# Expert layer of a three-stage kernel: token blocks in threes with a 15-product scheme in place of pairs with an 11-product scheme

## The chip, the cores and the metric

The kernel runs on one core of a Trainium2 chip. The metric is the device time of one execution in microseconds (us); less is better. The engines are named as in the profile: PE (TensorE matmuls) and PEld (its weight loads), DVE (VectorE), ACT (ScalarE), POOL (GpSimd), SP (the queue that issues the loads and stores).

## The reference

Three layers follow each other on 3072 tokens of width 384: a gated linear attention, a squared-ReLU MLP, and a layer of 8 experts mixed by a Sinkhorn-normalised gate. The change lies in the last one:

```python
def _moe2_ref(x, w_gate, w1, w2):          # x 3072x384, w1 8x384x1024, w2 8x1024x384
    logits = x @ w_gate
    P = np.exp(logits - logits.max())
    for _ in range(8):
        P /= P.sum(1, keepdims=True) + 1e-09
        P /= P.sum(0, keepdims=True) + 1e-09
        P *= N / E
    for e in range(E):
        h = np.maximum(x @ w1[e], 0.0)
        out += P[:, e:e + 1] * (h @ w2[e])
    return out
```

## The kernel before

Everything is laid out with features on the 128 partitions and tokens along the free axis. Attention runs in 24 chunks of 128 tokens, the MLP in 8 blocks of 384 tokens; both are interleaved, and each MLP result is stored to DRAM (`x2d`). The expert layer then takes the tokens in 3 pairs of blocks of 512 (`TB`), and for each pair all 8 experts. An expert has 1024 hidden features, taken in 4 steps of 256 (two blocks of 128). A step is numbered g, 96 in all; two steps make a super step q, 48 in all.

Each fp32 factor is split into a high part and the rest (`hi` by a cast on ACT, `lo` by a subtraction on DVE), and one block product (128x128 weights by 128x512 tokens) is three matmuls: hi·hi, hi·lo, lo·hi (`triple`, line 730).

First products (x by w1): a step needs 2 token blocks x 3 blocks of the width x 2 hidden blocks = 12 block products. A bilinear scheme (a Strassen-like one, `PROD`) does it with 11, on sums and differences of blocks of x (`x_sum`, once for a pair of token blocks) and of w1 (`w_sum` on POOL, lines 702 to 704, once a step). Its results are shared among outputs. So a PSUM bank is read while its sum is not finished (`take`, a copy by ACT, line 748), the next product is added to the same bank, and `part` and `whole` (DVE, lines 752 and 757) add the snapshots to the other banks. The finished hidden block goes through ReLU into `hi` (`hid_hi`, ACT, line 765) and `lo` (`hid_lo`, DVE, line 770).

Second products (h by w2, `second`, line 781): at the end of a super step, six groups (2 token blocks x 3 blocks of the output width) of 12 matmuls, each group summed in one of two PSUM banks. `weigh` (DVE, line 804) multiplies a finished group by the gate, `gather` (POOL, line 813) adds it to the accumulator in SBUF, which is stored after the last expert.

The weights of a step come by two loads (`ldwa`, `ldwc`) into two raw buffers; `w2_hi` (ACT, line 715) and `w2_lo` (DVE, line 719) split them. For the tokens, `ldx` loads a block from `x2d`; `x_hi` (line 678) and `x_lo` (line 681) split the blocks and the sums. The Sinkhorn steps (lines 1043 to 1062, DVE, POOL and a small matmul) run beside the first super steps; the gate is needed only from the second expert on, and the first expert's accumulators are scaled afterwards by `scale0` (POOL, line 807).

The order on every engine is fixed when the program is built: each operation is a step with an engine, a duration, a due time and its needs (`add`), and `Plan.order` plays them through and writes the instructions down in that order. At run time each engine executes its list in order and waits, by semaphores, for what the next instruction needs; nothing overtakes.

Of the kernel before, what the change touches and what calls it, by code (L numbers as in the profile page):

```python
# [37 lines left out]
NPAIR = NT // (2 * TB)  # L38
NST = NEF // 2
W1C = 10  # L40
WCOL = 2 * D
LAG = 2
NWP = 10
WARM_AT = 1.3
WARM_MARGIN = 0.45
W_AT = 6.0
CV_AT = 14.0
# [20 lines left out]
class Plan:  # L68
# [9 lines left out]
    def __init__(self):  # L78
        self.steps = {}

# [8 lines left out]
    def order(self):  # L89
# [11 lines left out]
        def arm(n):  # L101
            eng, _, due, _, needs, _, start = steps[n]
            at = max([ends[d] + (0.0 if steps[d][0] == eng else self.HOP) for d in needs] + [start])
            ready.setdefault(eng, []).append((at, due, n))
# [5 lines left out]
        while any(ready.values()):  # L110
            best = None
            for eng, c in ready.items():
                if not c:
                    continue
                t = max(free.get(eng, 0.0), min(x[0] for x in c))
                at, due, n = min((x for x in c if x[0] <= t), key=lambda x: (x[0] if eng == "dma" else x[1], x[0], str(x[2])))

                soon = min((x[0] for x in c if t < x[0] < t + min(steps[n][1], self.LOOK.get(eng, 0.0)) and x[1] + self.URGENT < due), default=t)
                if soon > t:
                    t = soon  # L120
                    at, due, n = min((x for x in c if x[0] <= t), key=lambda x: (x[1], x[0], str(x[2])))
                if best is None or t < best[0]:
                    best = (t, eng, (at, due, n))
# [4 lines left out]
            ends[n] = free[eng] + steps[n][5]  # L128
# [9 lines left out]
    def emit(self, between=None):  # L138

        free = 0.0  # L140
        for n in self.order():
            eng, dur, _, fn, _, lag, _ = self.steps[n]
            if eng == "pe" and between:
                at = self.ends[n] - lag - dur
                between(free, at)
                free = at + dur
            fn()


def body(tc, fkq, v, wm, wa, wc, gate, seqs, out):  # L150
# [8 lines left out]
    ps_e = ctx.enter_context(tc.tile_pool(name="ps_e", bufs=2, space=PSUM))  # L159
# [18 lines left out]
    right = ExitStack()  # L178
    rpool = lambda name, bufs: right.enter_context(tc.tile_pool(name=name, bufs=bufs, side="right", reuse_waits="tile"))
    wb = rpool("wb", 1)  # L180
    x1p = rpool("x1p", 2)
# [353 lines left out]
    def products_in(i, w, xx):  # L535
        ps = eps[i] = ps_e.tile([128, BT], F32, tag="e1", name="e1")
# [88 lines left out]
    NSTEP = NPAIR * NE * NST  # L625
    NSUP = NSTEP // 2

    def close_right():
# [6 lines left out]
        pools["pb"] = new("pbp", 2, side="right")  # L635
        pools["c"] = new("ps_c", 1, space=PSUM)
        pools["o"] = new("ps_o", 2, space=PSUM)
        pools["xr"] = new("xrp", 1, side="right")
# [6 lines left out]
    T_E1, T_E2 = 7.5, 16.3  # L645
# [6 lines left out]
    X, xr, x2r = {}, {}, {}  # L652

    def ldx(p, t):
        x2r[p, t] = pools["xr"].tile([128, KD, TB], F32, tag=f"x{t}", name="xraw") if p else rawp.tile([128, KD, TB], F32, tag="raw", name="xraw")
        lo, hi = (2 * p + t) * TB, (2 * p + t + 1) * TB
        while lo < hi:
            j = lo // BT
            end = min(hi, (j + 1) * BT)
            o = (2 * p + t) * TB  # L660
            sp.dma_start(out=x2r[p, t][:, :, lo - o:end - o], in_=x2d[j][:, :, lo - j * BT:end - j * BT])
            lo = end

# [12 lines left out]
    def x_hi(p, n):
        X.setdefault(p, {})[n] = (pools["xr"] if n == 0 and p == 1 else pools["x"]).tile([128, 2, (3, 2, 4)[n], TB], F32R, name="xd" if n == 0 and p == 1 else f"x{n}")
        act.copy(out=X[p][n][:, 0], in_=x_src(p, n))

    def x_lo(p, n):  # L680
        dve.tensor_tensor(out=X[p][n][:, 1], in0=x_src(p, n), in1=X[p][n][:, 0].bitcast(F32), op=ALU.subtract)

    def xop(p, name):
        n, k = {"a11": (0, 0), "a12": (0, 1), "a13": (0, 2), "a22": (1, 0), "a23": (1, 1),
                "s1": (2, 0), "s2": (2, 1), "s3": (2, 2), "s4": (2, 3)}[name]
        return [X[p][n][:, l, k, :] for l in range(2)]


    W2 = {}

    def ldwa(g):
        raws["a", g] = rawp.tile([128, W1C, 128], F32, tag="raw", name="rawa")
        sp.dma_start(out=raws["a", g][:, 0:6], in_=wa[g % (NE * NST)])

    def ldwc(g):
        raws["c", g] = rawp.tile([128, WCOL], F32, tag="raw", name="rawc")
        sp.dma_start(out=raws["c", g], in_=wc[g % (NE * NST)])

    def w_sum(g):
        r = raws["a", g]  # L700

        pool.tensor_tensor(out=r[:, 6:8], in0=r[:, 1:3], in1=r[:, 0:2], op=ALU.subtract)  # L702
        pool.tensor_tensor(out=r[:, 8], in0=r[:, 2], in1=r[:, 6], op=ALU.subtract)
        pool.tensor_tensor(out=r[:, 9], in0=r[:, 3], in1=r[:, 8], op=ALU.subtract)  # L704

    def w2src(g, k):
        if k == "c":
            return raws["c", g], WCOL
        r = raws["a", g].rearrange("p a b -> p (a b)")
        return (r[:, 0:WCOL], WCOL) if k == "a" else (r[:, WCOL:], 512)  # L710

    def w2_hi(g, k):
        W2[g, k] = wpool.tile([128, 2, WCOL], F32R, tag=f"w{(3 * g + 'abc'.index(k)) % NWP}", name="w2")
# [7 lines left out]
    def wop(g, name):  # L721
        c = {"b11": 0, "b22": 2, "b21": 3, "b13": 4, "b23": 5, "t1": 6, "t3": 7, "t2": 8, "t4": 9}[name]
        w, c = (W2[g, "a"], c) if c < 6 else (W2[g, "b"], c - 6)
        return [w[:, l, c * 128:(c + 1) * 128] for l in range(2)]

    bank, snap, vs, hs = {}, {}, {}, {}

    def triple(ps, w, x, start, stop):
        for n, (a, b) in enumerate(((0, 0), (0, 1), (1, 0))):
            pe.matmul(ps, w[a], x[b], start=start and n == 0, stop=stop and n == 2, skip_group_check=True)  # L730


    PROD = {"p1": ("a", (("b11", "a11"),)), "p2": ("b", (("b21", "a12"), ("b13", "a13"))),
            "p6": ("a", (("t2", "s2"),)), "p5": ("c", (("t1", "s1"),)), "p3": ("d", (("b22", "s4"), ("b23", "a13"))),
            "p7": ("a", (("t3", "s3"),)), "p22": ("c", (("b23", "a23"),)), "p4": ("e", (("t4", "a22"), ("b13", "a23")))}

    def product(g, name):
        k, ops = PROD[name]
        p = g // (NE * NST)
        fresh = name in ("p1", "p2", "p5", "p3", "p4")  # L740
        if fresh:
            bank[g, k] = ps_e.tile([128, TB], F32, tag="e1", name="e1") if k in "ab" else pools["c"].tile([128, TB], F32, tag=k, name="e2")
        for n, (w, x) in enumerate(ops):
            triple(bank[g, k], wop(g, w), xop(p, x), fresh and n == 0, True)

    def take(g, n):
        snap[g, n] = pools["x"].tile([128, TB], F32, tag=f"s{n}", name=f"s{n}")
        act.copy(out=snap[g, n], in_=bank[g, "a"])  # L748

    def part(g):  # L750
        vs[g, "t"] = pools["v"].tile([128, TB], F32, tag="t", name="t")
        dve.tensor_tensor(out=vs[g, "t"], in0=bank[g, "c"], in1=snap[g, 2], op=ALU.add)  # L752

    def whole(g, k):
        other = {"b": lambda: snap[g, 1], "d": lambda: vs[g, "t"], "c": lambda: snap[g, 3], "e": lambda: snap[g, 3]}[k]()
        vs[g, k] = pools["v"].tile([128, TB], F32, tag="v", name="v", bufs=3)
        dve.tensor_tensor(out=vs[g, k], in0=bank[g, k], in1=other, op=ALU.add)  # L757

    TF = {"b": (0, 0), "d": (0, 1), "c": (1, 1), "e": (1, 0)}

    def hid_hi(g, k):
        t, f = TF[k]
        f += 2 * (g % 2)
        hs[g // 2, t, f] = pools["h"].tile([128, 2, TB], F32R, tag=f"h{t}{f}", name="h")
        act.activation(out=hs[g // 2, t, f][:, 0], in_=vs[g, k], func=ACTF.Relu)  # L765

    def hid_lo(g, k):
        t, f = TF[k]
        h = hs[g // 2, t, f + 2 * (g % 2)]
        dve.scalar_tensor_tensor(out=h[:, 1], in0=vs[g, k], scalar=0.0, in1=h[:, 0].bitcast(F32), op0=ALU.max, op1=ALU.subtract)  # L770

    acc, ob, sc, pbt = {}, {}, {}, {}

    def second(q, t, m):
        ob[q, t, m] = pools["o"].tile([128, TB], F32, tag="o", name="o")
        for f in range(4):
            w = W2[2 * q + f // 2, "c"]
            c = (f % 2) * D + m * 128
            h = hs[q, t, f]
# [481 lines left out]
```

## Time and profile before

| | |
|---|---|
| three timed runs | 2098.16, 2093.79, 2095.75 us; median 2095.75 |
| profiled execution, first to last instruction | 2092.6 us |
| PE busy | 2059.8 us (98%), 10558 matmuls |
| DVE busy | 1308.6 us (63%) |
| ACT busy | 882.4 us (42%) |
| POOL busy | 640.9 us (31%) |
| mean granted TensorE clock | 0.994 of full speed |

The page gives no other time of the profiled execution than its span; the three timed runs lie 1.2 to 5.6 us above it. A busy time is the union of the records of an engine's instructions. A matmul's record (389 ns for 512 columns) is longer than the distance from one matmul to the next, because they overlap; the distance is read from stretches with a known number of matmuls.

### The profile page before, as it was taken

The page shows a single profiled execution, that of the slowest core. Times are in us where ns is not written, and L with a number is a line of the kernel's source. Part 1 is how long each engine was busy: PE and PEld are TensorE (multiplying, and loading weights), DVE is VectorE, ACT ScalarE, POOL GpSimd, SP SyncE. Part 2 cuts the span into 40 slices and gives each one's busy share as a digit, 9 for nine tenths or more (in the row PEclk, how much of TensorE's full clock was granted, in tenths as well). Part 3 has the DMA queues.
Part 4 walks back from the last instruction along what each step waited for, and adds up shares of the span by engine and source line. Part 5 has one row for each costly group of instructions (what it writes and reads, how often), then busy time and mean ns, then how long its engine had stood idle before and what let it go on. Part 6 is the DMA issues. An engine that isn't in the chain of part 4 may idle for free.

```text
span 2092.6 us, 27588 instructions
## 1 busy us (share of the span) xinstructions
PE 2059.8 (98%) x10558; PEld 1732.4 (83%) x10558; DVE 1308.6 (63%) x1999; ACT 882.4 (42%) x1519; POOL 640.9 (31%) x647
## 2 busy tenths in 40 slices
PE   8889999999999999999999999999999999999998
PEld 5579999999977888888888888888888888888887
DVE  8963444332576665667675665667666665665665
ACT  5644544445643343343343343343343343343341
POOL 4420111100124333334332333334332333333331
PEclk9999999999999999999999999999999999999999
DMA  7522222210212211121221111212112211111210
GB/s 284 176 74 66 78 89 70 69 32 18 87 31 78 71 56 56 61 86 56 71 86 56 61 56 56 71 56 86 61 56 86 71 56 56 61 56 56 71 46 32
DMA packets 55114, 148.75 MB, mean 71 GB/s; under 512 B 6333, under 2 KB 15549, under 8 KB 54973
## 3 DMA queue, kind: packets, MB, share of 16 engines
q1 hardware_dynamic: 54972, 146.90, 21.9%
q8 instruction: 85, 1.39, 0.3%
q14 instruction: 57, 0.46, 0.1%
HBM read 135.28 MB, written 9.54 MB: 69 GB/s over the span
## 4 chain that ended last, share of the span: by engine, by line
PE 91%; DVE 6%; DMA 1%; ACT 1%; issue 1%; POOL 0%; SPq 0%; DVEq 0%; POOLq 0%; ACTq 0%
PE o L781 36%; PE e L730 33%; PE e L544 9%; PE a L573 8%; PE pp L360 1%; PE y L408 1%; PE lg L588 1%; DVE h L770 1%; DVE cv_t L1006 1%; PE y L416 1%; DVE cv_t L1002 1%; DVE cv_t L998 1%; DVE w L298 1%; PE ds L382 1%; DVE w L719 1%; DMA rawa<-in_wa_dram 1%
## 5 line engine op out<-in xcount | busy, mean ns | idle before, releaser
L781 PE MATMUL o<-h,w 128*128 128x512 f32 x3456 | 799.0, 391 | 6.9 <-DVE sc L804 3.9
L781 PEld LDWEIGHTS o<-h,w 128*128 128x128 f32 x3456 | 649.3, 188 | 146.2 <-DVE sc L804 6.6
L730 PE MATMUL e<-x,w 128*128 128x512 f32 x2784 | 648.0, 389 | 0.0
L730 PEld LDWEIGHTS e<-x,w 128*128 128x128 f32 x2784 | 522.1, 188 | 108.3 <-DVE t L752 0.2
L748 ACT COPY s<-e 128x512 f32<-128x512 f32 x288 | 169.1, 587 | 842.5 <-PE e L730 837.6
L813 POOL TENSOR_TENSOR acc<-acc,sc 128x512 f32<-128x512 f32 x258 | 336.6, 1313 | 499.8 <-DVE sc L804 499.7
L804 DVE TENSOR_TENSOR sc<-o,pb 128x512 f32<-128x512 f32 x264 | 181.9, 689 | 372.6 <-PE o L781 341.2
L770 DVE SCALAR_TENSOR_TENSOR h<-v,h 128x512 fp32r<-128x512 f32 x384 | 278.2, 743 | 1.3 <-ACT h L765 1.1
L765 ACT ACTIVATE h<-v 128x512 fp32r<-128x512 f32 x384 | 242.5, 632 | 40.2 <-DVE v L757 40.1
L757 DVE TENSOR_TENSOR v<-e,s 128x512 f32<-128x512 f32 x288 | 198.0, 687 | 78.2 <-ACT w L715 61.5
L702 POOL TENSOR_TENSOR rawa<-rawa 128x256 f32<-128x256 f32 x96 | 79.7, 830 | 506.9 <-DMA rawa<-in_wa_dram 301.9
L544 PE MATMUL e<-x,w 128*128 128x384 f32 x1008 | 198.1, 339 | 0.0
L560 DVE TENSOR_TENSOR lo<-g,hi 128x384 fp32r<-128x384 f32 x112 | 65.6, 585 | 202.1 <-ACT hi L556 201.5
L544 PEld LDWEIGHTS e<-x,w 128*128 128x128 f32 x1008 | 173.9, 188 | 4.8 <-issue 2.4
L573 PE MATMUL a<-hi,w 128*128 128x384 f32 x672 | 171.9, 336 | 0.0
L719 DVE TENSOR_TENSOR w<-rawa,w 128x768 fp32r<-128x768 f32 x192 | 160.1, 834 | 6.3 <-ACT w L715 6.3
L715 ACT CAST w<-rawa 128x768 fp32r<-128x768 f32 x192 | 135.3, 729 | 22.1 <-POOL rawa L704 9.3
L549 ACT ACTIVATE g<-e 128x384 f32<-128x384 f32 x128 | 62.9, 491 | 160.5 <-PE e L544 148.8
L573 PEld LDWEIGHTS a<-hi,w 128*128 128x128 f32 x672 | 120.6, 188 | 0.9
L344 POOL TENSOR_TENSOR kq<-kq,sg 128x512 f32<-128x512 f32 x24 | 31.7, 1322 | 273.7 <-DVE sg L334 135.0
L573 PE MATMUL a<-lo,w 128*128 128x384 f32 x336 | 112.4, 335 | 0.0
L730 PE MATMUL e<-xd,w 128*128 128x512 f32 x384 | 97.4, 389 | 0.0
(110 smaller groups left out, 1529.6 us busy)
## 6 DMA issues: line engine op xcount, KB each, us to landing
rawa<-in_wa_dram SPq DMA_DIRECT2D x96, 384.0 KB, 3.1
rawc<-in_wc_dram SPq DMA_DIRECT2D x96, 384.0 KB, 3.3
raw<-in_wm_dram SPq DMA_DIRECT2D x16, 768.0 KB, 5.4
pb<-ptd SPq DMA_DIRECT2D x24, 512.0 KB, 3.8
fraw<-in_fkq_dram SPq DMA_DIRECT2D x23, 512.0 KB, 4.4
kq<-in_fkq_dram SPq DMA_DIRECT2D x23, 512.0 KB, 4.2
vt<-in_v_dram SPq DMA_DIRECT2D x24, 192.0 KB, 4.7
x2d<-x2t SPq DMA_DIRECT2D x8, 576.0 KB, 2.8
```

The source lines that it names most:

```text
L544: pe.matmul(ps, w[wl][:, k * 128:(k + 1) * 128], xx[:, xl, k, :], start=n == 0, stop=n == 3 * KD - 1)
L573: pe.matmul(acc1[j][m], W[f][wl][:, D + m * 128:D + (m + 1) * 128], g, start=f == 0 and n == 0, stop=f == NF - 1 and n == 2)
L715: act.copy(out=W2[g, k][:, 0, 0:n], in_=src)
L719: dve.tensor_tensor(out=W2[g, k][:, 1, 0:n], in0=src, in1=W2[g, k][:, 0, 0:n].bitcast(F32), op=ALU.subtract)
L730: pe.matmul(ps, w[a], x[b], start=start and n == 0, stop=stop and n == 2, skip_group_check=True)
L748: act.copy(out=snap[g, n], in_=bank[g, "a"])
L757: dve.tensor_tensor(out=vs[g, k], in0=bank[g, k], in1=other, op=ALU.add)
L765: act.activation(out=hs[g // 2, t, f][:, 0], in_=vs[g, k], func=ACTF.Relu)
L770: dve.scalar_tensor_tensor(out=h[:, 1], in0=vs[g, k], scalar=0.0, in1=h[:, 0].bitcast(F32), op0=ALU.max, op1=ALU.subtract)
L781: pe.matmul(ob[q, t, m], w[:, a, c:c + 128], h[:, b], start=f == 0 and n == 0, stop=f == 3 and n == 2)
L804: dve.tensor_tensor(out=dst, in0=ob[q, t, m], in1=pbt[p, e][:, t * TB:(t + 1) * TB], op=ALU.mult)
L813: eng.tensor_tensor(out=acc[p, t, m], in0=acc[p, t, m], in1=sc[q, t, m], op=ALU.add)
```

## The change

A group is now three blocks of 512 tokens, so there are 2 groups, 64 steps and 32 super steps. A step needs 3 x 3 x 2 = 18 block products and makes them with 15. They form five chains: a chain is a PSUM bank that gets up to five products one after the other, and after each product its running sum is read before the next one is added. The reads (`READ`) are 3 copies by ACT and 10 additions or subtractions by DVE; four hidden blocks come out of these sums, two straight from a bank (`DIRECT`). For two of the six hidden blocks `lo` is made on POOL, after ACT has applied ReLU in place (`hid_relu`). Five banks serve the chains, a sixth joins from step 6 on (`lay_banks`). The second products are 9 groups of 12 matmuls, written down in two halves each, in the order of token blocks 0, 2, 1.

The sums of w1 blocks grow from 4 blocks of 128 columns to 11 (three instructions of 256 columns, one of 384, two of 128, on POOL), and the split of the weights from tiles of 768, 512 and 768 columns to three of 640 and one of 768. In all but the first three steps and the first step of a group, the split of an even step's weights waits until the last first product of the step before it. The sums of x blocks are 17 (9 on DVE, 8 on POOL) for a group, the splits 15 blocks; for the second group they wait for the last first product of the first one. Gate rows and some scratch tiles share buffers with others (`w9`, `xe`, `v2`, `v3`).

The planner: an operation marked soft gives way to any other that becomes ready within a short time, the lag of an operation counts only for other engines, and durations are changed.

```diff
-NPAIR = NT // (2 * TB)
+GRP = 3
+NGRP = NT // (GRP * TB)
...
-            ends[n] = free[eng] + steps[n][5]
+            ends[n] = free[eng]
...
-    ps_e = ctx.enter_context(tc.tile_pool(name="ps_e", bufs=2, space=PSUM))
+    ps_e = ctx.enter_context(tc.tile_pool(name="ps_e", bufs=1, space=PSUM))
...
+    PROD = (6, 7, 8, 14, 4, 9, 13, 11, 12, 10, 0, 2, 5, 3, 1)
+    CHAIN = {"c4": (6, 14), "c0": (7, 4, 11, 0, 3), "c2": (8, 9, 12, 2, 1), "c1": (13, 10), "c3": (5,)}
...
+    XSUM = (("6", 6, (1, 1), (2, 0), ALU.add), ("0", 0, (0, 1), 6, ALU.subtract), ("2", 2, (0, 0), 6, ALU.subtract),
...
+    X_POOL = ("14a", "14", "13a", "13", "10a", "10", "5a", "5")
...
+    def x_lo(p, o):
+        dve.tensor_tensor(out=x_dst(p, o, 1), in0=x_src(p, o), in1=x_dst(p, o, 0).bitcast(F32), op=ALU.subtract)
...
-        pool.tensor_tensor(out=r[:, 6:8], in0=r[:, 1:3], in1=r[:, 0:2], op=ALU.subtract)
-        pool.tensor_tensor(out=r[:, 8], in0=r[:, 2], in1=r[:, 6], op=ALU.subtract)
-        pool.tensor_tensor(out=r[:, 9], in0=r[:, 3], in1=r[:, 8], op=ALU.subtract)
+            tt(out=r[:, 6:8], in0=r[:, 1:3], in1=r[:, 0:1].to_broadcast([128, 2, 128]), op=ALU.subtract)
+            tt(out=r[:, 8:10], in0=r[:, 6:8], in1=r[:, 5:6].to_broadcast([128, 2, 128]), op=ALU.subtract)
+            tt(out=r[:, 10:12], in0=r[:, 8:10], in1=r[:, 4:5].to_broadcast([128, 2, 128]), op=ALU.add)
+            return
+        c = raws["c", g]
+        tt(out=c[:, 0:3], in0=r[:, 9:12], in1=r[:, 3:4].to_broadcast([128, 3, 128]), op=ALU.add)
+        tt(out=c[:, 3], in0=r[:, 0], in1=r[:, 5], op=ALU.add)
+        tt(out=c[:, 4], in0=c[:, 1], in1=r[:, 2], op=ALU.add)
...
+    def product(g, o):
+        c = CHAIN_OF[o]
+        if o == CHAIN[c][0]:
+            bank[g, c] = new_bank(g, c)
+        x, w = X[g // GST, o], wop(g, o)
         for n, (a, b) in enumerate(((0, 0), (0, 1), (1, 0))):
+            pe.matmul(bank[g, c], w[a], x[:, b], start=o == CHAIN[c][0] and n == 0, stop=n == 2, skip_group_check=True)
+
+    READ = (("k", 6, "act", 0.49), ("t1a", 7, "dve", 0.61), ("t2a", 8, "act", 0.49), ("t2b", 4, "dve", 0.61), ("t2c", 14, "dve", 0.61),
+            ("t1b", 9, "dve", 0.61), ("t3a", 13, "act", 0.49), ("t0a", 11, "dve", 0.61), ("t0b", 12, "dve", 0.61), ("t0c", 10, "dve", 0.61),
+            ("t3b", 0, "dve", 0.61), ("t3c", 2, "dve", 0.61), ("t1c", 5, "dve", 0.61))
+    OUT = {2: "t2c", 0: "t0c", 3: "t3c", 1: "t1c"}
+    DIRECT = {5: 3, 4: 1}
+    H_POOL = (2, 3)
...
+        else:
+            t = vs[g, name[:2]]
+            op = ALU.subtract if name in ("t2b", "t1b", "t0a", "t0b") else ALU.add
+            dve.tensor_tensor(out=t, in0=t, in1=c, op=op)
...
+    def hid_lo(g, o):
+        h = hs[hid(g, o)]
+        if o in H_POOL:
+            pool.tensor_tensor(out=h[:, 1], in0=hid_src(g, o), in1=h[:, 0].bitcast(F32), op=ALU.subtract)
+        else:
+            dve.scalar_tensor_tensor(out=h[:, 1], in0=hid_src(g, o), scalar=0.0, in1=h[:, 0].bitcast(F32), op0=ALU.max, op1=ALU.subtract)
...
+    T_ORDER = (0, 2, 1)
+    TM = [(t, m) for t in T_ORDER for m in range(KD)]
...
+            needs.append(("p", g1, PROD[-1]) if p else "left")
...
+            if g > 2 and g % 2 == 0 and g % GST:
+                free = [free, ("p", g - 1, PROD[-1])]
...
+            if i:
+                needs.append(("read", g, of_op[CHAIN[c][i - 1]]))
...
+            add(("p", g, o), "pe", 0.68, at(u + 0.68 * j), lambda g=g, o=o: product(g, o), needs, FILL)
```

## Rows read from the trace of the kernel before

**Rows 1.** The page: engines' busy us and shares; chain that ended last, by line.

```profile
PE 2059.8 (98%) x10558; PEld 1732.4 (83%) x10558; DVE 1308.6 (63%) x1999; ACT 882.4 (42%) x1519; POOL 640.9 (31%) x647
...
PE o L781 36%; PE e L730 33%; PE e L544 9%; PE a L573 8%; PE pp L360 1%; PE y L408 1%; PE lg L588 1%; DVE h L770 1%; DVE cv_t L1006 1%; PE y L416 1%; DVE cv_t L1002 1%; DVE cv_t L998 1%; DVE w L298 1%; PE ds L382 1%; DVE w L719 1%; DMA rawa<-in_wa_dram 1%
```

**Rows 2.** Chain of one super step, 700 to 740 us: start, length, what, matmuls.

```profile
706.28 14.96 PE e L730 x66
721.24 16.32 PE o L781 x72
```

**Rows 3.** Groups by line: instructions, busy us, mean ns, idle before.

```profile
L781 PE MATMUL o<-h,w 128*128 128x512 f32 x3456 | 799.0, 391 | 6.9 <-DVE sc L804 3.9 <-DVE acc L798 2.4 <-DVE h L770 0.3
L730 PE MATMUL e<-x,w 128*128 128x512 f32 x2784 | 648.0, 389 | 0.0
L730 PE MATMUL e<-xd,w 128*128 128x512 f32 x384 | 97.4, 389 | 0.0
```

**Rows 4.** Stretches: PE, PEld, DVE, ACT, POOL busy us (instructions), then PE clock.

```profile
706.12:721.08 14.96, 14.96 (x68) 12.39 (x67) 12.96 (x19) 10.81 (x19) 3.60 (x4) 1.00 0.26 89
721.08:737.40 16.32, 16.32 (x74) 13.51 (x73) 7.57 (x12) 1.21 (x3) 8.04 (x8) 1.00 0.14 48
...
616.14:638.42 22.28, 19.80 (x85) 15.48 (x84) 14.10 (x28) 4.32 (x7) 7.22 (x10) 0.92 0.27 76
...
653.38:674.84 21.46, 18.34 (x74) 14.42 (x73) 11.56 (x12) 1.22 (x3) 13.74 (x11) 0.92 0.19 61
...
1065.15:1082.58 17.43, 16.92 (x73) 13.36 (x72) 11.82 (x14) 3.87 (x5) 9.57 (x8) 1.00 0.33 105
```

**Rows 5.** Instructions in order, first products: start, length, engine, operation, [idle before].

```profile
706.12 15.12 PE L730 MATMUL e<-x,w 128*128 128x512 f32 x66
...
707.05 0.59 ACT L748 COPY s<-e 128x512 f32<-128x512 f32 x1 [15.56 <-PE e L730]
...
710.50 0.68 DVE L770 SCALAR_TENSOR_TENSOR h<-v,h 128x512 fp32r<-128x512 f32 x1
711.10 0.68 DVE L757 TENSOR_TENSOR v<-e,t 128x512 f32<-128x512 f32 x1
711.70 0.68 DVE L719 TENSOR_TENSOR w<-rawa,w 128x512 fp32r<-128x512 f32 x1
...
715.51 1.05 POOL L702 TENSOR_TENSOR rawa<-rawa 128x256 f32<-128x256 f32 x1 [7.07 <-DMA rawa<-in_wa_dram]
...
715.87 1.23 DVE L770 SCALAR_TENSOR_TENSOR h<-v,h 128x512 fp32r<-128x512 f32 x1
```

**Rows 6.** Durations of three lines: min/median/max ns.

```profile
L770 DVE SCALAR_TENSOR_TENSOR h<-v,h x384: 641/682/1777, 572.6 to 2071.0; 128x512 fp32r<-128x512 f32 x192
...
L813 POOL TENSOR_TENSOR acc<-acc,sc x258: 1279/1289/2207, 662.5 to 2055.5; 128x512 f32<-128x512 f32 x129
...
L671 DVE TENSOR_TENSOR xs<-xraw,xs x3: 684/1771/1775, 538.4 to 1452.7; 128x512 f32<-128x512 f32 x3
```

**Rows 7.** Instructions in order around two waits of PE.

```profile
619.35 3.01 PE L781 MATMUL o<-h,w 128*128 128x512 f32 x12
...
624.12 0.63 DVE L798 TENSOR_TENSOR acc<-o,acc 128x512 f32<-128x512 f32 x1
...
624.80 4.46 PE L781 MATMUL o<-h,w 128*128 128x512 f32 x12 [2.43 <-DVE acc L798]
...
650.24 10.11 POOL L807 TENSOR_TENSOR acc<-acc,pb 128x512 f32<-128x512 f32 x6
...
654.84 4.38 DVE L770 SCALAR_TENSOR_TENSOR h<-v,h 128x512 fp32r<-128x512 f32 x3
...
662.42 5.78 PE L781 MATMUL o<-h,w 128*128 128x512 f32 x18 [3.05 <-DVE sc L804]
```

**Rows 8.** Groups by line on POOL, the sums of weight blocks.

```profile
L702 POOL TENSOR_TENSOR rawa<-rawa 128x256 f32<-128x256 f32 x96 | 79.7, 830 | 506.9 <-DMA rawa<-in_wa_dram 301.9 <-ACT h L765 162.5 <-DVE v L757 18.8
...
L704 POOL TENSOR_TENSOR rawa<-rawa 128x128 f32<-128x128 f32 x96 | 46.6, 485 | 7.5
```

More of the change, by code (lines that the diff above doesn't have):

```diff
@@ L102, in arm @@
             eng, _, due, _, needs, _, start = steps[n]
-            at = max([ends[d] + (0.0 if steps[d][0] == eng else self.HOP) for d in needs] + [start])
+            at = max([ends[d] + (0.0 if steps[d][0] == eng else self.HOP + steps[d][5]) for d in needs] + [start])
             ready.setdefault(eng, []).append((at, due, n))
@@ new lines, in x_f32, with x_sum, x_src @@
+    def x_f32(p, o):
+        if o in X_OVER:
+            return xraw[p, 0][0][X_OVER[o]]
+        if (p, "t") not in X:
+            X[p, "t"] = x1e.tile([128, 6, TB], F32, tag="x1", name="xt")
+        return X[p, "t"][:, X_SLOT[o]]
+    def x_sum(p, n, eng):
+        _, o, a, b, op = XSUM[n]
+        part = lambda s: xraw[p, s[0]][0][s[1]] if isinstance(s, tuple) else x_f32(p, s)
+        eng.tensor_tensor(out=x_f32(p, o), in0=part(a), in1=part(b), op=op)
+    def x_src(p, o):
+        if o == "89":
+            return xraw[p, 1][1][:, 1:3]
+        if o in SINGLE:
+            t, k = SINGLE[o]
+            return xraw[p, t][0][k]
+        return x_f32(p, o)
@@ L733, in body @@
[L733 to L757, printed above, removed]
@@ L772, in body, with wop @@
-    acc, ob, sc, pbt = {}, {}, {}, {}
[L774 to L779, printed above, removed]
-            for n, (a, b) in enumerate(((0, 0), (0, 1), (1, 0))):
-                pe.matmul(ob[q, t, m], w[:, a, c:c + 128], h[:, b], start=f == 0 and n == 0, stop=f == 3 and n == 2)
+    def wop(g, o):
+        k, c = W_OP[o]
+        return [W2[g, k][:, l, c * 128:(c + 1) * 128] for l in range(2)]
@@ new lines, in body, with lay_banks @@
+    bank, vs, hs = {}, {}, {}
+    RING_AT = 6
+    BANK, FREED = {}, {}
+    def lay_banks():
+        order = ("c4", "c0", "c2", "c1", "c3")
+        now = dict(zip(order, (0, 1, 2, 3, 4)))
+        spare = None
+        last = {}
+        for g in range(NSTEP):
+            if g == RING_AT:
+                spare = 5
+            old = now
+            if spare is None:
+                now = {"c4": old["c4"], "c0": old["c1"], "c2": old["c3"], "c1": old["c0"], "c3": old["c2"]}
+            else:
+                now = {"c4": spare, "c0": old["c4"], "c2": old["c1"], "c1": old["c3"], "c3": old["c2"]}
+                spare = old["c0"]
+            if g == 0:
+                now = old
+            for c in order:
+                BANK[g, c] = now[c]
+                FREED[g, c] = last.get(now[c])
+                last[now[c]] = (g, c)
@@ new lines, in body @@
+        for name, o, eng, dur in READ:
+            needs = [("p", g, o), "right"]
+            if name in READ_AFTER:
+                needs.append(("read", g, READ_AFTER[name]))
+            if name == "k":
+                needs += [("hlo", g - 2, 0)] if g >= 2 else []
+                needs += row_done(1, 2, r) if p and r < 2 else []
+            if name == "t1a":
+                needs += [("hlo", g - 2, 1)] if g >= 2 else []
+                needs += row_done(1, 2, 2) if (p, r) == (1, 0) else []
+            if name in ("t2a", "t3a"):
+                needs += [("hlo", g - 1, 2 if name == "t2a" else 3)] if g else []
+                if g % 2 == 0 and g:
+                    needs += [("ac", g // 2 - 1, *TM[7 if name == "t2a" else 8])]
+            n = PROD.index(o)
+            if name in OUT.values() and name != "t3c":
+                plan.soft.add(("read", g, name))
+            add(("read", g, name), eng, dur, at(u + 0.68 * n + 0.7), lambda g=g, name=name: read(g, name), needs, TAIL)
```

429 lines of the change are left out of this document (271 added, 158 removed).

## The prediction

> **What bounds the kernel now.** I read the page first. PE is busy 98% of the span, no other engine above 63%, and the two lines of the expert layer hold 69% of the chain that ended last [rows 1]. A busy share is an average, so the next view is the chain itself in a quiet stretch: it runs on PE alone, 66 matmuls of first products in 14.96 us and 72 of second products in 16.32 us, with nothing between [rows 2]. That gives the price of a matmul: 31.28 / 138 = 0.2267 us (its record of 389 ns overlaps the next one). The groups by line say that PE never waited ahead of a first product and 6.9 us in all ahead of second ones [rows 3]. So a matmul taken out of the expert layer is worth 0.2267 us as long as the others still keep up, and the whole question is whether they do. DVE is the one to look at: during the first products it is busy 12.96 of 14.96 us, 87%, with POOL at 3.60, 24% [rows 4].
>
> **What is removed.** Before, 96 steps of 11 products of 3 matmuls are 3168, as counted (2784 + 384) [rows 3]. After, 64 steps of 15 products are 2880. The second products stay at 3456: 32 super steps x 9 groups x 12. All have 512 columns and their own weight load, as before, so the price stays. 288 x 0.2267 = 65.3 us go, all from the path that sets the end. A step's first products then take 45 x 0.2267 = 10.2 us, a super step 20.4 + 24.5 = 44.9 us. The weight loads fall from 96 pairs to 64 and stay behind 3 to 4 us of landing in steps of 22 us; nothing is charged.
>
> **What is added to the chains.** A product that adds to a bank has to wait until the sum in it was read. In the new order two products, six matmuls, stand between each product and the next one of its chain. From the start of a product's last matmul to the start of that next one are 7 x 0.2267 = 1.59 us. The read needs: 0.39 for the matmul's record; 0.09 until the reader starts (first product of a step: its third matmul starts at 706.12 + 0.45, ends at 706.96, ACT starts at 707.05); 0.68 for a DVE read [rows 5]; 0.05 until PE goes on (DVE ends at 624.75, PE starts at 624.80) [rows 7]. Sum 1.21, so a slack of 0.38 us, if DVE is free. What is queued behind a late read is everything: the next product stands first in PE's list and nothing overtakes it.
>
> Back to back, DVE starts an instruction of 512 columns every 0.60 us (710.50, 711.10, 711.70) [rows 5], so it can follow reads that come every 0.68 us. In the first products of a super step it has 20 reads, 12.0 us, 8 rests of hidden blocks (`lo`), 4.8 us, and about one split of 768 weight columns, 0.60 x 1.5 = 0.9: 17.7 of 20.4 us, 87%, the same share at which PE did not wait before [rows 4]. The cover is thinner, though. From the fifth product to the thirteenth, reads come with every product but one and leave no hole of 0.6 us; the four `lo` of a step fit only around the turn from one step to the next, where DVE has six products, 4.1 us, for one read and four `lo`, 3.0 us. ACT has 6 copies, 12 ReLU into `hi` and 4 in place, at most 22 x 0.63 = 13.9 of 20.4 us, and is not the bound.
>
> **DVE beside POOL.** A `lo` that started at 715.87, inside a POOL instruction that ran from 715.51 to 716.56, took 1.23 instead of 0.68 us, and ended 0.54 after POOL's end: it did its work after POOL [rows 5]. Three `lo` beside `scale0` took 4.38 us [rows 7], and a sum of two SBUF operands has 1.77 against 0.68 us [rows 6]. The median `lo` shows nothing of it (682 ns), because POOL was rarely busy then. The change alters just that: in the first products of a super step POOL gets 4 `lo` x 1.29 = 5.2 us (length of its other 512-column operation [rows 6]), the weight sums of a step, 3 x 0.83 + 2 x 0.485 [rows 8] + 1.1 (384 columns, between 0.83 and 1.29) = 4.6, and two late accumulations, 2.6: 12.4 of 20.4 us, 61% instead of 24%.
>
> The Trainium skill (SBUF — State Buffer, "Who interferes with whom") says that VectorE and GpSimd share one pair of ports under an exclusive lock, that a VectorE instruction with two SBUF inputs contends with a GpSimd one that reads SBUF, and that the later one waits to the end. The trace agrees (1.23 us, above), and the rule speaks against this change, which puts more work on POOL. Taken at its worst for every `lo` it is the slow rival below.
>
> Price of a chain delay: a `lo` meets a busy POOL 0.61 of the time, has more than the slack left to wait in (1.29 - 0.38) / 1.29 = 0.70 of these cases, and then PE waits 0.46 us on average: 0.61 x 0.70 x 0.46 = 0.2 us. Per super step four DVE `lo` have both inputs in SBUF. All among the tight reads gives 0.8 us; as they are soft and mostly land at the turns, I take 0.3: 32 x 0.3 = 10 us. Lower bound 0, as in the first products before; upper bound, each meets a whole POOL instruction, 4 x 0.91 x 32 = 116 us.
>
> The `lo` that POOL makes: the block out of the twelfth product needs a read 0.68, two ACT operations 0.63 + 0.6, POOL 1.29 and about 0.4 of hand-overs, 3.6 us, and is asked for 3 products (2.0), half a group (1.4) and five matmuls (1.1) later, 4.5. If POOL is in a weight sum, the 0.9 of slack is just used up. I take 0.1 a super step, 3 us, between 0 and 0.5 x 32 = 16.
>
> The weight splits of an even step now wait for the end of the first products. Behind them on ACT and DVE stand only late ReLUs and `weigh` (9 x 0.60 and 8 splits of 0.75 to 0.9 are 11.7 of 24.5 us), so this costs nothing; without that cover the next step's first product would wait.
>
> **The turn to the second group.** 9 sums and 15 splits of x on DVE (24 x 0.60 = 14.4), 8 sums on POOL (10.3), and besides 4 weight splits (3.2), 9 accumulations (11.6) and weight sums (4.6). All of these have two SBUF inputs or run on POOL: 44.1 us if they exclude each other strictly. There are 24.5 us of second products plus 12 products, 8.2, until the last operands are needed: 32.7. So between 0 and 11.4 us late. I take 7, nearer to exclusion as the rows above show it. The two turns of before cost 17.43 - 16.32 = 1.1 us each [rows 4] and go: +5 net, between -2 and +12 (with the reload of a weight buffer that the tokens now borrow).
>
> **The start.** Beside Sinkhorn PE waited 2.43 us, and 3.05 us after `scale0` had held up DVE; the granted clock was 0.92 in both stretches, and the 12 matmuls behind the first wait took 4.46 instead of 3.01 us [rows 4, 7]. After, `scale0` has 9 pieces of 1.69, 15.2 us, beside chains that are tighter, but the gate is needed only after 90 us instead of 63. +2, between -5 and +15. The end is the same chain of last group, `weigh`, sum and store: 0.
>
> **Sum.** -65.3 + 10 + 3 + 5 + 2 = -45.3. Against the profiled span, 2092.6 - 45.3 = 2047.3; the median of the timed runs lies 3.15 above that span, so 2050.
>
> **Rivals.** (1) Nothing waits: the plan knows the DVE and PE distances to 0.01 us, and PE did not wait at 87% before. 2095.75 - 65.3 = 2030, down to 2025 if the start's waits vanish too. Against it: POOL at 61%. (2) DVE's list falls behind in each step: 0.8 x 32 = 26, a strict turn +9, start +10, POOL's `lo` +5: -15, 2080. (3) Slower: POOL's instructions hold up `lo` among the tight reads in every step, 116 us as above, +9 and +10 for turn and start: 2095.75 + 70 = 2165. It decides from 65.3 / 64 = 1.02 us of waiting a step on; against it, the soft order keeps most `lo` out of the tight stretch. That the change does less than it says cannot be: the tables give 45 matmuls a step.
>
> **How the numbers follow.** A measurement of this kernel can tell about 0.2% (4 us) from no change. Forecast, 2038 to 2066: 0.48. Rival 1: 0.22. Rival 2, 2066 to 2091: 0.13. Within 0.2%: 0.05. Rival 3: 0.12. So faster 0.83, same 0.05, slower 0.12. The range takes in rival 1's 2030 and most of rival 2: 2028 to 2088.
>
> **What would show it.** A super step of about 45.2 us in the chain, 44.9 without waits; first products of two steps in 20.4 to 21; waits of PE on DVE reads (the banks' names) of 0.1 to 0.9 us each, and `lo` of 1 us and more beside POOL. At the turn, waits of PE on x splits. Wrong if a super step is above 46 us, if PE waits for ACT's copies, or if the turn or the start alone costs over 20 us.

## The result: 2062 us, 1.6% less

The changed kernel takes 2062.06 us (2060.24 to 2062.98, four runs) against 2094.77 for the kernel before beside it: ratio 0.984, interval 0.9826 to 0.9855. That is 33 us less where 45 were forecast and 65 were taken out. One execution among all those below (of the run without additions in the quiet stretches) took 2085.75 us at a granted clock of 0.923, a slower state of the chip, and is left out of its median. The profiled execution took 2060.24 us, its span is 2058.2. The page, to set beside [rows 1] (engine shares; the slices of PE and of the granted clock):

```profile
PE 2014.1 (98%) x10270; PEld 1676.1 (81%) x10270; DVE 1399.2 (68%) x2024; ACT 895.4 (44%) x1541; POOL 976.1 (47%) x884
...
PE   8989999999999999999999999799999999999998
...
PEclk9999999999999999999999999899999999999999
```

PE has 288 matmuls less and is as full as before, but for one slice in the middle, where its clock falls too: the turn from the first group to the second. In a quiet stretch the chain looks like this (start, length, what, matmuls; to set beside [rows 2]):

```profile
763.95 20.72 PE e L838 x90
784.67 24.49 PE o L900 x108
809.16 20.74 PE e L838 x90
829.90 24.48 PE o L900 x108
```

The second products keep the old distance, 24.49 / 108 = 0.2268 us. The first products should take 90 x 0.2267 = 20.40 and take 0.3 us more. The stretches of a quiet super step and of the last one before the turn (columns as in [rows 4]):

```profile
809.00:829.74 20.74, 20.74 (x92) 16.64 (x90) 17.79 (x27) 10.70 (x19) 7.67 (x8) 1.00 0.06 19
829.74:854.22 24.48, 24.48 (x110) 20.27 (x108) 15.23 (x20) 7.54 (x12) 19.74 (x18) 1.00 0.15 49
1261.22:1288.05 26.83, 23.00 (x92) 17.46 (x90) 24.14 (x33) 15.92 (x26) 11.18 (x12) 0.94 0.20 62
1288.05:1327.92 39.87, 29.40 (x110) 22.95 (x108) 36.68 (x37) 11.46 (x18) 28.11 (x20) 0.83 0.26 91
```

From the first product of the expert layer to the end I take from each such stretch its matmuls x 0.2267. What is over (us; the first row is a time from the start of the span):

| stretch | before | after |
|---|---|---|
| first product starts at | 562.63 | 567.74 |
| first three super steps | 18.4 | 16.3 |
| turns between groups and single waits (before), the one turn (after) | 3.3 | 6.4 + 15.4 |
| other super steps | 0 | 9.4 |
| after the last group | 6.9 | 6.8 |

The differences are +5.1, -2.1, +18.5, +9.4 and -0.1; with -65.3 they make -34.5, and the spans differ by 34.4. So 30.8 of the 65.3 us were lost again, and 18.5 of these at the turn. There POOL, DVE and PE look like this (start, length, instruction, count; in brackets PE's wait):

```profile
1294.18 0.68 DVE L924 TENSOR_TENSOR sc<-o,pb 128x512 f32<-128x512 f32 x1
...
1295.49 3.38 DVE L733 TENSOR_TENSOR xt<-xraw,xt 128x512 f32<-128x512 f32 x2
1296.58 1.74 POOL L733 TENSOR_TENSOR xt<-xraw 128x512 f32<-128x512 f32 x1
...
1300.47 3.41 DVE L753 TENSOR_TENSOR x<-xraw,x 128x512 fp32r<-128x512 f32 x2
...
1301.74 4.93 POOL L733 TENSOR_TENSOR xt<-xt,xraw 128x512 f32<-128x512 f32 x3
...
1305.47 0.68 DVE L924 TENSOR_TENSOR sc<-o,pb 128x512 f32<-128x512 f32 x1
...
1306.21 8.17 PE L900 MATMUL o<-h,w 128*128 128x512 f32 x24 [7.09 <-DVE sc L924]
...
1317.64 10.44 PE L900 MATMUL o<-h,w 128*128 128x512 f32 x36 [3.27 <-DVE sc L924]
```

Ten of the 22 sums and splits on DVE last about 1.7 us instead of 0.68 and two 1.15; the other ten keep 0.68. The eight sums on POOL last 1.59 to 1.74 instead of 1.29: where both engines are at work, they go in turns. `weigh` (0.68 us, one operand in PSUM) stands behind seven of the sums and splits in DVE's list, from 1294.18 to 1305.47, so a bank of the second products stays full and PE waits 7.09 and then 3.27 us. The 24 matmuls after the first of these waits took 8.17 us instead of 24 x 0.2267 = 5.4, part of them at the lower level of the clock, 1.2 GHz. So of the 15.4 us 10.4 are waits and the other 5.0 slower matmuls behind them.

### The profile page after: what moved, and what is told of

Same layout as the page of the kernel before. It is cut to its first block, busy times and chain, and to the rows that moved or that the text cites. A ratio compares the mean times of both kernels' runs of the same rounds, so it can differ in the third digit from the quotient of the medians.

```text
span 2058.2 us, 27262 instructions
## 1 busy us (share of the span) xinstructions
PE 2014.1 (98%) x10270; PEld 1676.1 (81%) x10270; DVE 1399.2 (68%) x2024; ACT 895.4 (44%) x1541; POOL 976.1 (47%) x884
## 4 chain that ended last, share of the span: by engine, by line
PE 91%; DVE 7%; DMA 1%; issue 1%; ACT 0%; POOL 0%; SPq 0%; DVEq 0%; POOLq 0%; ACTq 0%
PE o L900 37%; PE e L838 31%; PE e L554 9%; PE a L583 8%; PE y L418 1%; PE pp L370 1%; DVE x L753 1%; PE lg L598 1%; DVE cv_t L1204 1%; PE y L426 1%; DVE cv_t L1200 1%; DVE cv_t L1196 1%; DVE w L308 1%; PE ds L392 1%; DVE xt L733 1%
## 5 line engine op out<-in xcount | busy, mean ns | idle before, releaser
L900 PE MATMUL o<-h,w 128*128 128x512 f32 x3456 | 795.5, 391 | 10.5 <-DVE sc L924 10.4
L838 PE MATMUL e<-x,w 128*128 128x512 f32 x2304 | 543.4, 392 | 0.5 <-DVE vt L861 0.3
L838 PEld LDWEIGHTS e<-x,w 128*128 128x128 f32 x2304 | 425.0, 188 | 106.1 <-DVE vt L861 13.8
L884 POOL TENSOR_TENSOR h<-v,h 128x512 fp32r<-128x512 f32 x128 | 166.5, 1301 | 372.2 <-ACT v L879 372.2
L793 DVE TENSOR_TENSOR w<-rawc,w 128x640 fp32r<-128x640 f32 (+1 forms) x128 | 176.9, 1383 | 96.5 <-ACT w L789 96.3
L789 ACT CAST w<-rawc 128x640 fp32r<-128x640 f32 (+1 forms) x128 | 97.5, 787 | 287.5 <-PE o L900 194.4
L865 DVE TENSOR_TENSOR v<-v,e 128x512 f32<-128x512 f32 x256 | 174.6, 682 | 43.4 <-PE e L838 36.3
L554 PEld LDWEIGHTS e<-x,w 128*128 128x128 f32 x1008 | 175.1, 189 | 4.8 <-issue 2.4
L838 PE MATMUL e<-xr,w 128*128 128x512 f32 x576 | 146.4, 398 | 7.3 <-DVE h L886 5.6
L793 DVE TENSOR_TENSOR w<-rawa,w 128x640 fp32r<-128x640 f32 x128 | 122.8, 960 | 39.0 <-ACT w L789 39.0
L865 DVE TENSOR_TENSOR vk<-vk,e 128x512 f32<-128x512 f32 x192 | 131.9, 687 | 19.9 <-DVE vk L865 1.4
L838 PEld LDWEIGHTS e<-xr,w 128*128 128x128 f32 x576 | 108.1, 191 | 34.4 <-DVE h L886 6.5
```

What stands on the lines that cost most here:

```text
L554: pe.matmul(ps, w[wl][:, k * 128:(k + 1) * 128], xx[:, xl, k, :], start=n == 0, stop=n == 3 * KD - 1)
L789: act.copy(out=W2[g, k][:, 0, 0:n], in_=src)
L793: dve.tensor_tensor(out=W2[g, k][:, 1, 0:n], in0=src, in1=W2[g, k][:, 0, 0:n].bitcast(F32), op=ALU.subtract)
L838: pe.matmul(bank[g, c], w[a], x[:, b], start=o == CHAIN[c][0] and n == 0, stop=n == 2, skip_group_check=True)
L865: dve.tensor_tensor(out=t, in0=t, in1=c, op=op)
L884: pool.tensor_tensor(out=h[:, 1], in0=hid_src(g, o), in1=h[:, 0].bitcast(F32), op=ALU.subtract)
```

## The experiments

All times are medians beside runs of the kernel before (2095.5 to 2095.7 us). In the profiled runs the attention ends up to 8 us earlier or later (first MLP product at 121.8 to 129.6 us), so pieces are compared by their own lengths; "over" means over matmuls x 0.2267. The turn is not the same in every trace of the changed kernel either: 21.8 us over in the one above, 24.1 in its second one (shown at the end of this section). So differences of 2 us at the turn between single traces are not read. The planner orders every engine's list anew after an edit; where a list stayed the same, the text says so.

**Without the second group's preparation.** The loops over groups that load, add and split the tokens run for the first group only:

```diff
-        x, w = X[g // GST, o], wop(g, o)
+        x, w = X[0, o], wop(g, o)
...
-    for p in range(NGRP):
+    for p in range(1):
```

> Left out: the second group takes the operands of the first one, so its token loads, 17 sums and 15 splits are not made. Theory (the preparation of the second group's tokens is what costs at the turn): the 21.8 us that PE loses there in the trace of the changed kernel go but for 1 us, so about 2041 us. Rival (the turn costs by its output stores, gate rows or accumulators): 10 us or more of the loss stay, 2052 us or more.

2045.59 us (2041.98 to 2046.39). The last second products are 0.36 us over instead of 15.4, the last first products still 4.1 instead of 6.4:

```profile
1261.28:1285.79 24.51, 21.76 (x91) 16.40 (x90) 21.97 (x30) 13.41 (x23) 11.87 (x14) 1.00 0.16 49
1285.79:1310.63 24.84, 24.77 (x109) 20.19 (x108) 12.53 (x16) 4.42 (x8) 15.02 (x13) 1.00 0.26 91
```

So with the tokens' preparation 17.3 of the 21.8 us go, more than the spread of the turn, and 4.1 come from something else in the first products. The edit also lifts waits for buffers that the tokens share with gate rows and weights; in the changed kernel PE's waits at the turn are all for DVE.

**The same, and the weight splits of the second group's first step wait like those of the others.**

```diff
-            if g > 2 and g % 2 == 0 and g % GST:
+            if g > 2 and g % 2 == 0:
```

> Left out, as in the run that takes the first group's operands for the second one: loads, sums and splits of the second group's tokens. Besides, the weight splits of the second group's first step wait for the end of the first products as those of any even step do. Theory (the 4.1 us that the last first products before the turn still lose there come from these four splits among the tight reads): the loss falls to 0.3 us: 4 us faster than that run, 2041 us. Rival (POOL's lo and weight sums make it): 3 us or more stay, 2045 us.

2041.57 us (2040.02 to 2043.79). The stretch falls from 24.51 to 20.72 us, the second products stay at 24.48:

```profile
1266.43:1287.15 20.72, 20.72 (x91) 16.61 (x90) 17.85 (x27) 10.70 (x19) 7.67 (x8) 1.00 0.07 20
1287.15:1311.63 24.48, 24.48 (x109) 20.28 (x108) 15.00 (x20) 7.54 (x12) 18.70 (x17) 1.00 0.32 106
```

The 4.1 us go, as the theory had it, when the four weight splits leave the tight reads. Six weight sums of POOL left the stretch with them (8 instructions instead of 14), so this run does not quite separate the splits from the rival. With no preparation and these splits later the turn costs nothing.

**POOL's sums at the turn as copies by ACT.** DVE keeps its instructions, but part of their order changes.

```diff
+        if p and XSUM[n][0] in X_POOL:
+            act.copy(out=x_f32(p, o), in_=part(a))
+            return
```

> Changed in its result: at the turn the eight sums of POOL become copies of one operand, made by ACT; the list of DVE keeps its instructions. Theory (POOL and DVE exclude each other, so that at the turn each DVE operation on two SBUF operands takes 1.7 us instead of 0.68): the loss at the turn falls from 21.8 to 8 to 12 us, about 2050 us, and the sums and splits of DVE show 0.7 us wherever no accumulation of POOL runs beside them. Rival (DVE simply has too much work there): nothing changes, 2062 us within 3.

2053.21 us (2051.0 to 2054.41). The second products at the turn are 8.4 us over instead of 15.4, with 29.17 us of DVE instead of 36.68:

```profile
1287.02:1319.92 32.90, 27.05 (x109) 21.01 (x108) 29.17 (x37) 15.83 (x29) 16.37 (x13) 0.95 0.32 102
```

Around PE's first wait:

```profile
1294.19 0.68 DVE L927 TENSOR_TENSOR sc<-o,pb 128x512 f32<-128x512 f32 x1
...
1300.11 0.68 DVE L927 TENSOR_TENSOR sc<-o,pb 128x512 f32<-128x512 f32 x1
...
1300.83 4.41 PE L903 MATMUL o<-h,w 128*128 128x512 f32 x12 [2.78 <-DVE sc L927]
```

DVE was busy 7.5 us less in the stretch with 37 instructions in both, because eight others on POOL were gone: exclusion; the rival falls. Up to the first wait DVE's list is the same as before: seven sums and splits between two `weigh` take 5.92 us instead of 11.29, and PE waits 2.78 us instead of 7.09. Behind it the `weigh` stand earlier in the list (6, 4 and 4 operations between them instead of 1, 9 and 5), so part of the fall from 15.4 to 8.4 belongs to the order. The whole turn is 13.8 us over (5.4 + 8.4), a little above the 8 to 12 of the forecast.

**Besides, no additions by POOL in the last super step of the first group.**

```diff
-        if e or s:
+        if (e or s) and q != NSUP // 2 - 1:
             eng.tensor_tensor(out=acc[p, t, m], in0=acc[p, t, m], in1=sc[q, t, m], op=ALU.add)
```

> Changed in its result: as the run with POOL's sums at the turn made copies by ACT, and POOL's additions in the last super step of the first group are left out too. Theory (exclusion is what is left of the 8.4 us in the second products at the turn): DVE's 33.0 us there fall to about 25, the loss to 0 to 3 us, about 2047 us. Rival (DVE's own work is too long for 24.5 us): 6 us or more stay, 2051 us or more.

2049.21 us (2048.16 to 2050.64):

```profile
1289.97:1318.52 28.55, 26.66 (x109) 20.70 (x108) 23.92 (x37) 15.12 (x28) 4.25 (x5) 0.96 0.40 112
```

DVE falls to 23.92 us, 4.1 us over remain, between the two forecasts. DVE's list is the same as in the run before, so the fall from 8.4 to 4.1 is exclusion. (The 33.0 us of the expectation are the length of the stretch; DVE was busy 29.17 of it.) The two runs together take 11.3 of the 15.4 us, by exclusion and, in the first, by the order. The rest is there even with POOL nearly still; that it comes from DVE's own work, which all but fills the 24.5 us, was not shown.

**All sums on DVE, in both groups.**

```diff
-    X_POOL = ("14a", "14", "13a", "13", "10a", "10", "5a", "5")
+    X_POOL = ()
```

> All 17 sums of each group on DVE, none on POOL. Theory (exclusion): DVE gets 8 x 0.60 = 4.8 us more to do at each of the two places and still ends earlier: the loss at the turn falls from 21.8 to 12 to 15 us, the 5 us by which the expert layer starts later than in the kernel before fall to 1 to 3: 2050 us. Rival (too much work on DVE): 4 to 5 us more at the turn and 0 to 3 at the start, 2067 us.

2056.7 us (2053.51 to 2060.91). The expert layer starts 438.7 us after the first MLP product, as in the kernel before (123.91 to 562.63), and no longer 443.2 (124.49 to 567.74): 4.5 of the 5.1 us of the later start; the rest is the attention. At the turn the products are 5.6 + 13.5 = 19.1 over, not the 12 to 15 of the forecast:

```profile
1283.50:1321.48 37.98, 27.80 (x110) 21.81 (x108) 34.12 (x45) 12.13 (x21) 16.37 (x13) 0.87 0.27 85
```

Around PE's first wait:

```profile
1290.65 0.68 DVE L924 TENSOR_TENSOR sc<-o,pb 128x512 f32<-128x512 f32 x1
...
1301.02 0.68 DVE L924 TENSOR_TENSOR sc<-o,pb 128x512 f32<-128x512 f32 x1
...
1301.76 8.13 PE L900 MATMUL o<-h,w 128*128 128x512 f32 x24 [7.22 <-DVE sc L924]
```

DVE does 45 instructions in 34.12 us, 37 took 36.68 before, so DVE is the better place for these sums. But PE's first wait is as long as before, 7.22 us, though most of what stands ahead of it now has 0.68 us: 14 sums and splits stand between the two `weigh` instead of seven. So the order of DVE's list is a cause beside exclusion. An order with `weigh` ahead of the preparation was not run, and what it would give back is open.

How the late start came about is to be read in the changed kernel's trace, while the last MLP blocks run:

```profile
515.25 4.88 POOL L733 TENSOR_TENSOR xt<-xt,xraw 128x512 f32<-128x512 f32 x3
515.51 3.48 DVE L753 TENSOR_TENSOR x<-xt,x 128x512 fp32r<-128x512 f32 x2
...
518.92 1.76 DVE L733 TENSOR_TENSOR xraw<-xraw 128x512 f32<-128x512 f32 x1
...
520.61 1.61 DVE L570 TENSOR_TENSOR lo<-g,hi 128x384 fp32r<-128x384 f32 x1
...
522.28 0.44 PE L583 MATMUL a<-lo,w 128*128 128x384 f32 x1 [2.33 <-DVE lo L570]
```

The sums and splits of the first group, held up by POOL, stand ahead of the MLP's own `lo`, which takes 1.61 instead of 0.56 us, and PE waits 2.33 us for it.

**Besides, the four blocks that need no sum are split after the first products.**

```diff
-                needs = [("ldx", (p, 1 if o == "89" else 2))] + [("p", g1, c) if p else "left" for c in ((8, 9) if o == "89" else (o,))]
+                needs = [("ldx", (p, 1 if o == "89" else 2)), ("p", g1, PROD[-1]) if p else "left"]
```

Until then the splits of these blocks waited only for the products that use the old ones; that all of them wait for the last first product, as the description of the change has it, holds for those that need a sum.

> As the run with all sums on DVE, and in the second group the splits of the four blocks that are used without a sum (4, 7, 8, 9) wait for the last first product of the first group. Theory (the 6.4 us lost in the last first products before the turn come from DVE's list, where a split that waits for a token load stands ahead of the reads): these go, at most 2 us come back in the second products: 4 to 6 us faster than that run, 2045 us. Rival (those 6.4 us are exclusion by POOL as well): as that run, within 2 us.

2055.63 us (2052.93 to 2058.75), as the run before. The last first products are 3.8 over instead of 5.6, the second ones 15.0 instead of 13.5: at most moved, not saved. The order explains 1.8 of the 6.4 us at most; 4.1 went with the weight splits above.

**DVE adds in the last super step of the first group.**

```diff
-        eng = dve if q == NSUP - 1 else pool
+        eng = dve if q in (NSUP // 2 - 1, NSUP - 1) else pool
```

> As the run with all sums on DVE, and in the last super step of the first group DVE adds to the accumulators too, instead of POOL. Theory (exclusion): DVE gets 9 x 0.60 = 5.4 us more, but the nine additions no longer hold it up for 1.2 us each; the loss in the second products at the turn falls from 13.5 to 9 to 11 us: 3 us faster than that run, 2054 us. Rival (only DVE's work counts): 5 us slower than that run, 2062 us.

2052.83 us (2051.72 to 2054.76), ratio 0.9801 (0.9785 to 0.9817): the lowest median of the kernels that leave nothing out, just below the theory's 2054; the rival's 2062 falls. The second products at the turn are 12.1 us over instead of 13.5, less of a gain than the 2.5 to 4.5 expected, and within the spread of the turn:

```profile
1282.29:1318.91 36.62, 28.19 (x109) 22.15 (x108) 34.71 (x53) 12.16 (x21) 5.08 (x5) 0.86 0.30 103
```

POOL is down to 5 us, DVE does eight more instructions in about the same time and is full. What is gained by taking POOL away goes into DVE's own work.

**The quiet stretches: no additions by POOL**, but for the first super steps and the last experts.

```diff
-        if e or s:
+        if (e or s) and (e == NE - 1 or q < 2 * NST // 2):
```

> Left out: POOL's additions to the accumulators, but for the first super steps and the last expert of each group; all else is done. Theory for the 0.3 us a super step in the quiet stretches (the split of 768 weight columns takes 1.8 instead of 0.95 us, because an addition of POOL holds it up; so the last weighing and the first read of the next step come late, and PE waits before the fifth product): with the addition gone the split has 0.95 us and the first products of a pair of steps fall from 20.68 to 20.40 to 20.50 us; 4 to 7 us in all over some 24 super steps, about 2056 us. Rival (the order of DVE's list and the hand-overs make the wait, POOL has no part): 20.68 us stay, 2062 us.

2056.5 us (2053.65 to 2058.5, three runs), near the theory's 2056. DVE's list is the same as in the changed kernel. The excess of the first products falls from 0.28 to 0.36 to 0.15 us in most super steps, all quiet ones together from 9.4 to 5.6. What stands ahead of the fifth product, in the changed kernel:

```profile
761.96 2.54 POOL L933 TENSOR_TENSOR acc<-acc,sc 128x512 f32<-128x512 f32 x2
...
763.50 1.81 DVE L793 TENSOR_TENSOR w<-rawc,w 128x768 fp32r<-128x768 f32 x1 [1.47 <-ACT w L789]
...
765.24 0.68 DVE L924 TENSOR_TENSOR sc<-o,pb 128x512 f32<-128x512 f32 x1
...
765.84 0.67 DVE L861 TENSOR_TENSOR vt<-vk,e 128x512 f32<-128x512 f32 x1
...
766.56 5.31 PEld L838 LDWEIGHTS e<-x,w 128*128 128x128 f32 x24 [0.32 <-DVE vt L861]
```

and without the additions, one place of that kind:

```profile
896.27 0.96 DVE L793 TENSOR_TENSOR w<-rawc,w 128x768 fp32r<-128x768 f32 x1 [1.54 <-ACT w L789]
897.15 0.68 DVE L924 TENSOR_TENSOR sc<-o,pb 128x512 f32<-128x512 f32 x1
898.19 0.69 DVE L861 TENSOR_TENSOR vt<-vk,e 128x512 f32<-128x512 f32 x1 [0.36 <-PE e L838]
```

The split falls from 1.81 to 0.96 us, and the first read now waits for PE, not PE for it. So half of the 0.3 us is exclusion by POOL's additions, and these lines show where; the other half, 0.15 us, was not taken apart.

**That split later.** As the kernel in which DVE adds in the last super step of the first group, and the 768-column split of an odd step waits until the last sum of the step before is read.

```diff
+            if k == "c" and g % 2 and g > 2:
+                free += [("read", g - 1, "t1c")]
```

> As the run with all sums on DVE and DVE adding in the last super step of the first group; besides, the split of the second-product weights of an odd step (768 columns) waits until the last sum of the step before is read, so it no longer stands before the first reads of the even step. Theory (that split, held up by POOL, makes the wait before the fifth product): first products of two steps fall from 20.7 to 20.45 to 20.6 us, 3 to 6 us faster than that run, 2048 us. Rival (the split is only moved and holds up other reads): same as that run or slower, 2053 to 2060 us.

2102.9 us, ratio 1.0039 (1.0026 to 1.0051): 7 us above the kernel before, and 50 above the run that it is to be compared with. The theory fails. The first products are down to 20.47 us (with 25 instructions of DVE in them instead of 27), but the second ones rise to 26.36:

```profile
810.73:831.20 20.47, 20.47 (x92) 16.88 (x90) 16.36 (x25) 9.85 (x17) 6.79 (x7) 1.00 0.06 20
831.20:857.56 26.36, 25.04 (x109) 20.12 (x108) 17.34 (x21) 8.31 (x14) 20.33 (x19) 1.00 0.16 45
```

PE waits there for ReLUs and `lo` that are now late:

```profile
833.31 0.73 PE L900 MATMUL o<-h,w 128*128 128x512 f32 x2 [0.60 <-ACT h L876]
...
834.77 2.56 PE L900 MATMUL o<-h,w 128*128 128x512 f32 x10 [0.72 <-DVE h L886]
```

The whole order of DVE and ACT was written anew around the later split, and the second products' first operands came out last. Which of the moved instructions makes them late was not isolated.

**All `lo` on DVE.**

```diff
-    H_POOL = (2, 3)
+    H_POOL = ()
```

> All six rests of the hidden blocks (lo) on DVE, none on POOL. Theory (DVE's list is full in the first products, so that POOL's share of the lo is worth its price): DVE gets 4 x 0.60 = 2.4 us more in the 20.4 us of first products of a super step, 95% at back-to-back pace; first products of two steps rise from 20.7 to 21.2 to 22.5 us: 2075 to 2115 us. Rival (POOL's lo cost as much by exclusion as they save): 20.7 us stay, 2062 us within 4.

2065.53 us (2062.57 to 2067.68), against 2062.29 (2058.54 to 2064.81) for the changed kernel on the same chip:

```profile
810.53:830.93 20.40, 20.40 (x92) 16.89 (x90) 17.83 (x28) 8.27 (x15) 5.00 (x5) 1.00 0.06 20
830.93:855.83 24.90, 24.79 (x110) 20.19 (x108) 17.47 (x23) 7.44 (x12) 17.73 (x17) 1.00 0.16 48
```

The total is the rival's (2062 within 4), but neither account fits. The planner put only one of the four `lo` of a super step into the first products (28 instructions of DVE instead of 27) and three into the second ones (23 instead of 20). So DVE's busy time hardly changes in the first (17.83 against 17.79 us) and rises in the second (17.47 against 15.23): 2.28 us for four `lo`, 0.57 each, nearly their full price of 0.60. The first products lose nothing, and a wait of 0.4 us for a `lo` appears in the second ones. What four more `lo` in the first products would cost was not tested.

**Five banks only.** `RING_AT = 10 ** 9` instead of 6.

> The sixth PSUM bank never joins the chains; they run on five banks all the time, as in the first six steps. Theory (a product waits only for reads of its own chain): no change, 2062 us within 2. Rival (the first products of a step wait for a bank whose last sum is still unread): first products of two steps rise by 0.5 us or more, 2075 us or more.

2062.91 us (2062.34 to 2064.45) beside 2062.29: no change. The sixth bank gives nothing back, so a wait for a free bank is no part of the 0.3 us.

**The changed kernel again.**

> The changed kernel once more, beside the next three on one chip, to compare them with: 2062 us within 2.

2062.29 us (2058.54 to 2064.81), as expected. Its turn, with every list unchanged:

```profile
1263.72:1291.51 27.79, 23.47 (x91) 17.74 (x90) 24.59 (x33) 15.71 (x26) 11.96 (x12) 0.91 0.20 60
1291.51:1332.72 41.21, 29.91 (x109) 23.59 (x108) 34.77 (x37) 11.45 (x18) 30.51 (x20) 0.81 0.22 73
```

That is 7.4 + 16.7 = 24.1 us over, against 6.4 + 15.4 = 21.8 in the trace of the result.

## Why the prediction came out as it did

The forecast was 2050 us, 2038 to 2066 set apart from the rivals and 2028 to 2088 with them, and the kernel takes 2062: inside both. The 288 matmuls, their price and that they come off the path were right: second products keep 0.2268 us, first products of two steps come within 0.3 us of 90 x 0.2267, and a super step is 45.2 us, as named. The chains and POOL's `lo` were put at 13 us and cost 9.4. The size was right by luck, for the place was not: the steps priced `lo` between tight reads, beside a POOL that is busy 61% of the first products. It is busy 37% (7.67 of 20.74 us), and the runs show a weight split ahead of the first reads, held up by an addition of POOL, for half of the excess. POOL's `lo` were put at 0.1 us a super step in the second products; in the changed kernel these lose 0.0.

The start was put at +2 and is +3.0: 5.1 us later and 2.1 us less inside. That too is luck: the place named, Sinkhorn and `scale0`, got better, and what cost was the preparation of the first group inside the MLP, which no step priced (4.5 us, gone with all sums on DVE).

The step that failed is the turn, +5 net with an end at +12, measured +18.5. By the prediction's own sign it was wrong there: the turn alone costs 21.8 us, over the 20 named. PE's waits were named as waits for x splits; they are waits for `weigh` behind sums and splits. The mechanism was in the text, exclusion of DVE and POOL on two SBUF operands, and the total it gave, 44.1 us, is not far from the 39.9 that the second products took. Four things made the size wrong. The step set against it 24.5 us of second products plus 8.2 of the first products after them; but DVE is 86% busy there (17.79 of 20.74 us), and the order has finished all the preparation before (the next first products are 0.2 us over). So only 24.5 count. It did not price that the weight splits of the group's first step are let into the tight stretch: 4.1 us. It took DVE's work as one sum and not as a list, in which `weigh` stands behind the preparation. And it left out the clock: with waits of 7.09 and 3.27 us the granted clock of the stretch was 0.83, part of the matmuls behind them ran at 1.2 GHz, and that is 5.0 of the 15.4 us. How much of the turn is exclusion and how much order is known only in part: 4.3 us fell with the list unchanged, 7.0 with part of it changed.

The Trainium skill's rule (SBUF — State Buffer, "Who interferes with whom"), that the later of the two engines waits to the end, is what the trace shows in pairs of 1.7 us.

The slow rival needed 1.02 us of waiting a step; the quiet steps have 0.16. The rival with DVE's list behind in each step put 0.8 us on a super step, which has 0.3, and a strict turn at +9, which is half of what was measured. The rival without waits, 2030, missed by 32 us: 18.5 of them are the turn, 9.4 the quiet steps and 3.0 the start.

## What to carry to other kernels

Price a preparation that comes once by the free time of the engine that makes it in the stretch where it must be made, not by PE's: a full DVE hides nothing. Count DVE operations on two SBUF operands and POOL operations in one sum; where it exceeds the stretch, moving POOL's part to DVE was a gain here, until DVE's own list was the bound. Look also at what stands ahead of the instruction that frees a PSUM bank: seven operations of mostly 1.7 us and 14 of mostly 0.68 us made PE wait as long. A list order that is written anew by a planner moves many instructions at once: look for the new wait before trusting a local edit.

## What the hardware showed that was not expected

Held up in turns, neither engine keeps its own pace: POOL's sums of 512 columns rose from 1.29 to between 1.59 and 1.74 us while DVE's rose from 0.68 to 1.7, so that a pair costs about 1.7 us, little less than both one after the other (1.97). `weigh`, which has one operand in PSUM, kept its 0.68 us beside a busy POOL (1305.47). And what an operation costs when it goes from POOL to DVE depends on what POOL held up with it: at the turn DVE with eight more sums was busy 34.12 us instead of 36.68, in the quiet steps four more `lo` a super step cost it 2.28 us, 0.57 each.
